# Half-array attention matmuls and seven 256-token Strassen blocks in a fused attention and FFN kernel

## The chip, the cores and the metric

The kernel runs on one core of one Trainium2 chip, as one program in one launch. The metric is the device time of that program in microseconds. A core has TensorE (PE in the profile; its weight loads are listed apart as PEld), VectorE (DVE), ScalarE (ACT), GpSimd (POOL) and SyncE (SP, which issues the DMAs here). PE writes its results to PSUM, eight banks of 128 partitions by 512 float32 numbers.

## The reference, cut to what matters

```python
# q, k, v: (8 batches, 8 heads, 576 positions, 64) float32; omega: (128, 64)
def phi(x):                                   # random features
    proj = np.einsum('bhsd,md->bhsm', x, omega)
    sq = np.sum(x * x, axis=-1, keepdims=True) / 2.0
    h = proj - sq
    h = h - np.max(h, axis=-1, keepdims=True)
    return np.exp(h) / np.sqrt(m)
q_p, k_p = phi(q * scale), phi(k * scale)
kv  = np.einsum('bhsm,bhsd->bhmd', k_p, v)
z   = np.sum(k_p, axis=2)
num = np.einsum('bhsm,bhmd->bhsd', q_p, kv)
den = np.einsum('bhsm,bhm->bhs', q_p, z)[..., None] + 1e-06
x = (num / den)                               # -> 4608 tokens of 8*64 = 512
h = x @ w_in                                  # 512 -> 2048
g = 0.5 * h * (1.0 + erf(h / sqrt(2)))
out = g @ w_out                               # 2048 -> 512
```

All inputs and the output are float32. The term `sq` is the same for all features of a position, so it falls out when the maximum is taken off.

## The kernel before

**Attention units.** The 64 pairs of batch and head are worked off as 32 units of two heads (`units`, four per batch). Units 0 to 7 are plain: their matmuls take float32 operands (`pair`, `shared`, `kv`, `q_trans`, `num_plain`; L566, L573, L598, L636, L646). The other 24 units are split: an operand is kept as a high part and the rest, and products of parts are added. For a split unit, `load_dup` brings k and q in twice, so that one copy of a head's 64 dimensions lies in partitions 0 to 63 and one in 64 to 127, both heads side by side. `x_high` (L776, ACT) rounds all 128 partitions to float32r, and `x_low` (L785, POOL) replaces the lower 64 partitions by the rest. So one matmul over 128 rows adds high and low part. `proj` (L793) makes the features of k, nine matmuls of 256 columns (128 for each part of omega), which `proj_lo` (L797, ACT) and `proj_add` (L803, DVE) add up. `proj_q` (L815) makes those of q, eight matmuls of 288 columns. `q_blocks` (L818, L820), `exps` (L591), `q_back` (L851), `q_high` (L854) and `q_low` (L857) follow. `kv_split` (L897) makes kv and z in float16 parts. `num` (L655) makes numerator and denominator, twelve float32r matmuls of 288 columns per unit; one head's denominators come out above its numerators and the other's below, so `den` (L666, ACT) and `div` (L704, DVE) work on 64 partitions at a time, twice.

**FFN blocks.** The 4608 tokens go through the FFN in 13 blocks, `TBS` (L28): two of 256, ten of 384, one of 256. Block 0 takes float32 operands (L1076, L1102). In the others each product is three float16 matmuls (high by high, high by low, low by high). In a plain block, `mm1` (L1081) makes the hidden layer, 16 chunks of 12 matmuls with the block's tokens as columns, `gelu`, `g_high` (L1089, L1093, ACT) and `g_low` (L1097, DVE) make the parts of the result, and `mm2` (L1105 to L1107) multiplies by w_out, 48 matmuls of 512 columns for each 128 tokens. From block 9 on (`n0=9`: three of 384 tokens, one of 256), the first product is Strassen's in Winograd's form: seven products instead of eight of half the tokens by half the weights (`WHICH`, `w_prod`, L1294), with sums in PSUM (`c_sum`, L1307) and `w_mm2` (L1392 to L1394) for the second product. `w_prod` has half a block's tokens as columns, so 192 or 128.

**Order.** All operations are put into a `Planner`, which runs a list schedule with costs in microseconds, due times and tables of offsets (`STARTS`, `UDUE`, `OFF`), and emits one fixed order for each engine; an engine takes its instructions in that order. Attention units are fed in among the FFN blocks that come before the block that needs them. PSUM's eight banks are three rings: `acc` (three, second product), `h` (two, first product) and `at` (three, attention; in the Strassen blocks also their sums, `wr`).

Of the kernel before, what the change touches and what calls it, by code (L numbers as in the profile page):

```python
# [19 lines left out]
P = 128  # L20
T = 384
KSC = 2.0 ** 15
TINY = 1e-30
LAG = 2
TOP = 12
TBS = (256, 256) + (384,) * 10 + (256,)

X = dict(fb=1875.39, fbp=-594.94, fb0=-100.43, fbb=-85.01, fbw=8.75, pm=0.081, tsw=1.28, wmaxp=0, plain=8, kvp=8, eb0=8,  # L28
         ttr=1, pair=0, amax=63, qm=1, xm=0, km=0, prelu=0, n0=9, h=2, at=3, vs=5, wr=('h', 'at'), tx=4, ss=4, xh=8, gh=3,
         xp=0, qs=0)  # L30
# [3 lines left out]
STARTS = (-608.76, -310.19, 1013.97, 411.45, 613.3, 691.46, 1509.94, 850.35, 1239.92, 423.8, 1230.35, 1650.1, 1806.11,  # L34
          2438.49)
UDUE = (-1835.47, 171.94, -234.99, -505.01, 748.03, 1179.69, 3047.74, -146.1, -767.14, 900.21, 68.96, 2288.49, -294.59,
# [4 lines left out]
OFF = dict(b_high=-72.2, b_low=149.89, b_sum=1036.96, block_be=-107.12, block_high=221.4, block_low=-34.61,  # L41
           block_out=133.15, block_scales=552.27, block_spread=241.34, bound_a=61.51, bound_b=190.66, bound_c=-206.74,
           c_gelu=585.14, c_high=449.81, c_low=-623.5, c_low22=-1100.56, c_sum=205.13, chain_a=-306.63, chain_b=-159.63,
           chain_c=-20.0, chain_d=-212.25, den=17.46, div=-80.04, exp_tiles=752.95, exps=-624.6, g_high=-17.63,
           g_low=681.68, gelu=134.14, identity=-186.13, k_high=160.56, k_low=-326.52, k_shift=158.24, kv=-341.75,
           kv_a=-532.4, kv_b=-581.5, kv_b2=112.12, kv_c=86.33, kv_d=-195.75, kv_split=0.29, kvz_plain=362.33,
           load_dup=24.33, load_om=-374.68, load_two=-636.72, load_v=79.48, load_vst=733.3, mm1=151.18, mm2=960.95,
           nothing=772.2, num=-1.25, num_plain=152.14, p2=44.04, pair=30.95, proj=-73.32, proj_add=-20.84, proj_lo=-1064.92,
           proj_q=-79.55, q_back=299.04, q_blocks=91.52, q_copy=-909.26, q_high=70.66, q_low=-32.77, q_max=104.46,
           q_max2=-71.57, q_max3=-83.93, q_max4=-451.32, q_max5=-143.98, q_max6=390.66, q_shift=14.7, q_trans=-186.45,  # L50
           rcp=-223.48, s_high=197.71, s_low=-146.15, s_sum=214.23, s_sum2=35.14, scale_om=55.95, shared=-372.74,
           shift_tiles=-70.18, split_om=993.71, store=-152.29, store_dma=923.2, top=-95.1, v_a=100.77, v_b=111.57,
           v_max=90.81, v_scales=239.24, v_spread=-1125.26, w_abs=757.07, w_hi=-597.71, w_high=301.17, w_lo=320.3,
           w_load=239.07, w_low=35.09, w_max=36.92, w_mm2=-5.42, w_prod=11.49, w_round=138.68, w_seed=390.89,
           w_shift=-223.02, w_sign=-65.79, w_snap=253.45, warm=-115.6, wchain_a=0.47, wchain_b=-558.98, wchain_c=89.3,
           wchain_d=945.01, wchain_e=-544.08, wchain_f=348.34, x_high=-9.09, x_low=138.92, zeros=126.31)
# [7 lines left out]
class Planner:  # L64
# [45 lines left out]
    def run(self, lat, hop, alloc, put):  # L110
# [117 lines left out]
def favor_attention_ffn(ctx: ExitStack, tc: tile.TileContext, qT, kT, v, omT, w_in, w_out, out):  # L228
# [7 lines left out]
    TB = TBS  # L236
# [30 lines left out]
    ones = cp.tile([1, P], F32, name="ones")  # L267
    vta = cp.tile([P, 2, NV, D + 1], F32, name="vt")
# [8 lines left out]
    xf = xt.rearrange("p a h s -> p (a h s)")  # L277
# [10 lines left out]
    pair_at = [xsb[:, 0:2 * T], xsb[:, 2 * T:4 * T], flat0[:, VO:VO + 2 * T], flat0[:, VO + 2 * T:VO + 4 * T], xaf[:, 0:2 * T], xaf[:, 2 * T:4 * T]]  # L288
    pair_at += [w32f[:, 1, c:c + 2].rearrange("p c w -> p (c w)")[:, 0:2 * T] for c in (0, NF // 2)]
    pair_at = [t.rearrange("p (j t) -> p j t", j=2) for t in pair_at]  # L290
    tx_at = [flat0[:, VO + (4 + i) * T:VO + (5 + i) * T] for i in range(3)] + [xaf[:, 4 * T:5 * T]]
# [10 lines left out]
                vsc=2, bs=4, be=2, tx=X['tx'], ss=X['ss'], raw=2, r=2 if X['xm'] else 3, lo=2, qt=2, ql=2 if X['qm'] else 4, kvh=1, kvl=1, xh=X['xh'], xl=X['xh'], gh=X['gh'], gl=X['gh'], o=2)  # L302
    for k, b in bufs.items():
# [103 lines left out]
    def w_lo(pc):  # L407
        nc.scalar.activation(pc.l or raw(pc)[1], raw(pc)[1].bitcast(U32), AF.Copy, scale=2.0 ** -29)
# [78 lines left out]
    def weights_in(win, i):  # L487
# [4 lines left out]
        op('ACT', 1.08, w_lo, pc, r=[rk], w=pc.lk if pc.l is not None else [rk + ('lo',)])  # L492
# [13 lines left out]
    def weights_scale(win):  # L506
# [33 lines left out]
    def ek(u, t):  # L540
# [3 lines left out]
        return [('eq', u.eb, g) for g in range(a // HS, b // HS + 1)]  # L544
# [64 lines left out]
    def sums(u):  # L609
# [3 lines left out]
        if u.kp:  # L613
            pv = kv_out(u)
            return pv[:, :, 0:D], pv[:, :, D:D + 1]
        kz = G['kvz', u].rearrange("p a (b d) -> p (a b) d", d=D)
        return kz[:, 0:4:3], kz[:, 1:3, 0:1]

    def bound_a(u):
        nc.scalar.activation(G['zr', u], sums(u)[1], AF.Copy, bias=TINY)  # L620
# [909 lines left out]
```

## Time and profile before

| What | us |
|---|---|
| median of three runs | 984.22 (981.91 to 984.6) |
| profiled execution, its own time | 984.64 |
| its span, first to last instruction | 982.9 |
| TensorE busy in the span | 951.7 |
| VectorE busy | 768.7 |
| ScalarE busy | 764.7 |
| GpSimd busy | 419.5 |

The profiled execution's own time is 1.7 us above its span. Matmuls are pipelined: a row's duration runs from its start to its modelled end, and overlaps that of the next. What one matmul costs the engine is the distance from its start to the next one's start, read in the timeline. Each row of the timeline has its start, its length, engine, line and operation, what it writes and reads, then rows by columns of the array that are active, then partitions by columns and type. A float32 matmul of the program appears as two records, a float32r or float16 one as one.

### The profile page before, as it was taken

The numbers are of one execution on the slowest core, as the hardware profiler recorded it, in microseconds if no ns is written. First come the engines' busy times: TensorE is split into PE (matmuls) and PEld (weight loads), VectorE is DVE, ScalarE is ACT, GpSimd is POOL, SyncE is SP. The second block draws the span as 40 slices with busy tenths as digits, with TensorE's granted clock in tenths as the row PEclk, the third lists the DMA queues.
The fourth block names the chain that finished last, engine by engine and source line by source line (L and its number), as shares of the span: only waits on it lengthen the run. The fifth ranks groups of instructions, "written<-read, shape, count | busy, mean of one in ns | idle before, by whom it ended". The sixth has DMA issues, their size and how long they took to land.

```text
span 982.9 us, 18957 instructions
## 1 busy us (share of the span) xinstructions
PE 951.7 (97%) x6572; PEld 625.3 (64%) x6572; DVE 768.7 (78%) x2023; ACT 764.7 (78%) x1591; POOL 419.5 (43%) x612
## 2 busy tenths in 40 slices
PE   7988999899999999999999999999999999999998
PEld 5765666656655555565656665665666777767776
DVE  4898998999989997898889986996989575642322
ACT  6998768799899879979799987787779675654453
POOL 2235345666647674752564533552565011220000
PEclk7999999999999999999999999999999999999999
DMA  9774324222213221322213222231111000000000
GB/s 270 219 230 143 131 57 128 63 83 63 63 55 89 76 62 58 82 67 83 62 38 102 66 52 70 62 90 43 50 49 49 10 2 33 2 22 12 1 34 22
DMA packets 46287, 71.01 MB, mean 72 GB/s; under 512 B 13680, under 2 KB 22256, under 8 KB 46192
## 3 DMA queue, kind: packets, MB, share of 16 engines
q1 hardware_dynamic: 46192, 69.81, 24.1%
q8 instruction: 52, 0.85, 0.4%
q14 instruction: 43, 0.35, 0.1%
HBM read 60.36 MB, written 9.44 MB: 71 GB/s over the span
## 4 chain that ended last, share of the span: by engine, by line
PE 68%; DVE 18%; ACT 5%; POOL 3%; issue 2%; DMA 1%; SPq 1%; ACTq 0%; POOLq 0%
PE h L1081 16%; PE h L1294 5%; PE acc L1105 5%; PE acc L1107 5%; PE acc L1106 5%; PE at L1294 5%; PE acc L1393 4%; PE acc L1394 4%; PE acc L1392 4%; PE acc L1102 3%; PE at L655 3%; PE h L1076 2%; DVE gl L1097 2%; PE at L793 2%; PE at L897 2%
## 5 line engine op out<-in xcount | busy, mean ns | idle before, releaser
L785 POOL TENSOR_TENSOR r<-xt,r 64x288 fp32r<-64x288 f32 (+2 forms) x216 | 178.2, 843 | 147.0 <-ACT r L776 107.1
L1081 PE MATMUL h<-xh,wih 128*128 128x384 f16 (+1 forms) x512 | 163.7, 320 | 8.3 <-DVE gl L1097 7.6
L1081 PE MATMUL h<-xl,wih 128*128 128x384 f16 (+1 forms) x512 | 163.7, 320 | 0.0
L1081 PE MATMUL h<-xh,wil 128*128 128x384 f16 (+1 forms) x512 | 163.7, 320 | 0.0
L1105 PE MATMUL acc<-woh,gh 128*128 128x512 f16 x368 | 140.2, 381 | 0.0
L1107 PE MATMUL acc<-wol,gh 128*128 128x512 f16 x368 | 139.5, 379 | 0.0
L1106 PE MATMUL acc<-woh,gl 128*128 128x512 f16 x368 | 139.5, 379 | 0.0
L1081 PEld LDWEIGHTS <-wih 128*128 128x128 f16 x1024 | 97.6, 98 | 55.2 <-issue 0.2
L1097 DVE SCALAR_TENSOR_TENSOR gl<-h,bs,gh 128x384 f16<-128x384 f32 (+1 forms) x128 | 75.6, 590 | 24.9 <-ACT gh L1093 23.5
L776 ACT CAST r<-xt 128x256 fp32r<-128x256 f32 (+2 forms) x216 | 82.2, 407 | 15.6 <-PE at L815 6.8
L1089 ACT ACTIVATE h<-h,bs 128x384 f32<-128x384 f32 (+1 forms) x128 | 69.0, 540 | 25.3 <-PE h L1081 23.9
L1093 ACT ACTIVATE gh<-h,bs 128x384 f16<-128x384 f32 (+1 forms) x128 | 72.3, 566 | 13.1 <-PE acc L1107 9.8
L1081 PEld LDWEIGHTS <-wil 128*128 128x128 f16 x512 | 50.0, 98 | 39.2 <-issue 11.8
L1393 PE MATMUL acc<-woh,gl 128*128 128x512 f16 (+1 forms) x192 | 69.4, 361 | 0.1
L1392 PE MATMUL acc<-woh,gh 128*128 128x512 f16 (+1 forms) x192 | 69.4, 362 | 0.0
L1394 PE MATMUL acc<-wol,gh 128*128 128x512 f16 (+1 forms) x192 | 69.4, 361 | 0.0
L1294 PEld LDWEIGHTS <-w 128*128 128x128 f16 x768 | 60.3, 98 | 11.1 <-issue 0.9
L1107 PEld LDWEIGHTS <-gh 128*128 128x128 f16 x368 | 36.0, 98 | 43.4
L793 PE MATMUL at<-om,r 128*128 128x256 f32 x216 | 53.6, 337 | 2.6 <-POOL r L785 2.0
L1105 PEld LDWEIGHTS <-gh 128*128 128x128 f16 x368 | 35.8, 97 | 31.6 <-issue 0.2
L417 POOL TENSOR_TENSOR w<-w 128x1024 int32<-128x1024 int32 x12 | 28.5, 2375 | 61.9 <-DVE w L414 35.3
L1106 PEld LDWEIGHTS <-gl 128*128 128x128 f16 x368 | 36.1, 98 | 27.2 <-issue 0.3
(285 smaller groups left out, 2549.8 us busy)
## 6 DMA issues: line engine op xcount, KB each, us to landing
xt<-in_kT SPq DMA_DIRECT2D x56, 288.0 KB, 3.9
xt<-in_qT SPq DMA_DIRECT2D x56, 288.0 KB, 3.8
out_x<-o SPq DMA_DIRECT2D x35, 256.0 KB, 2.1
raw<-in_w_in SPq DMA_DIRECT2D x16, 512.0 KB, 5.5
raw<-in_w_out SPq DMA_DIRECT2D x16, 512.0 KB, 4.4
w<-in_v SPq DMA_DIRECT2D x24, 320.0 KB, 3.0
vt<-in_v SPq DMA_DIRECT2D x8, 320.0 KB, 4.7
out_x<-o SPq DMA_DIRECT2D x2, 128.0 KB, 1.7
```

Source lines behind the costliest of these rows:

```text
L776: nc.scalar.copy(G['r', u, x][:, 0:b - a], xf[:, a:b])
L785: nc.gpsimd.tensor_tensor(r, xf[D:, a:b], r, op=ALU.subtract)
L793: nc.tensor.matmul(o[:, t], r[:, t * P:(t + 1) * P], om, start=True, stop=True)
L1081: nc.tensor.matmul(h[:, 0:t], w, (G['xh', n, j], G['xh', n, j], G['xl', n, j])[k][:, 0:t], start=(i == 0), stop=(i == 3 * NJ - 1))
L1097: nc.vector.scalar_tensor_tensor(G['gl', n, c][:, 0:t], G['h', n, c][:, 0:t], G['bs', n][:, 3:4], G['gh', n, c][:, 0:t], op0=ALU.mult, op1 ...
L1105: nc.tensor.matmul(acc, gh[:, s], woh[:, c, c0:c1], start=(c == 0), stop=False)
L1106: nc.tensor.matmul(acc, gl[:, s], woh[:, c, c0:c1], start=False, stop=False)
L1107: nc.tensor.matmul(acc, gh[:, s], wol[:, c, c0:c1], start=False, stop=(c == NF - 1))
L1294: nc.tensor.matmul(b[:, g * h:(g + 1) * h], w, x[:, kt], start=first and k == 0, stop=last and k == 6 * GP - 1, skip_group_check=True)
L1392: nc.tensor.matmul(acc, gh, woh[:, c, c0:c1], start=begin, stop=False)
L1393: nc.tensor.matmul(acc, gl, woh[:, c, c0:c1], start=False, stop=False)
L1394: nc.tensor.matmul(acc, gh, wol[:, c, c0:c1], start=False, stop=end)
```

## The change

A split unit's two heads now lie on the two halves of the partitions, as they come from memory (`load_two` instead of `load_dup`), and the high and the low part in two tiles (`rh`, `rl`) of all 128 partitions. A projection's operands have 64 rows, so it takes one half of TensorE's rows, and the matmuls of the two heads are issued in turn, each head to a PSUM bank of its own. For k there are, per head, four matmuls of 256 columns (the high part by both parts of omega) and four of 128 (the low part by the high part of omega); the 64 positions per head that are left over are made in float32, in a quarter of the array (`proj_mid`). For q there are six of 288 columns per head. The numerators and denominators are made from float16 parts: each matmul has 64 weight columns, takes one half of the array's columns, and the heads are issued in turn; there are 24 of 288 columns per unit instead of 12. Numerators of both heads now fill one bank and denominators another, so `den` and `div` work on 128 partitions, once.

The FFN has blocks of 256, 256, six of 384 and seven of 256 tokens; the last seven are Strassen's, 1792 tokens where it was 1408. Their `w_prod` matmuls have 128 columns, and an operation on the sums takes four chunks (`GP = 4`) and 512 columns at a time. The parts of x have a buffer of their own (`xx`). The planner has new costs, offsets and a table `MOVES` of offsets for single operations, all of which set the order.

The diff, cut to its core (the tables, of which a program makes the order, are shown by their rows below):

```diff
-TBS = (256, 256) + (384,) * 10 + (256,)
+    KP = X['k']
+    N0 = 2 + KP
+    TB = (256, 256) + (384,) * KP + (256,) * ((NTOK - 512 - 384 * KP) // 256)
...
     def num(u, half):
-        for hh in range(2):
-            ps = G['pn', u, half, hh]
+        def one(hh, a):
+            o, w = G['pn', u, half, a][hh * D:(hh + 1) * D, 0:HS], slice(a * D, (a + 1) * D)
+            h, l = (G[z, u][:, hh, w] for z in ('kvh', 'kvl'))
             qh = G['qh', u][:, hh * S + half * HS:hh * S + (half + 1) * HS]
-            ops = [(G['kvh', u], qh), (G['kvl', u], qh), (G['kvh', u], G['ql', u, half][:, hh] if X['qm'] else G['ql', u, 2 * hh + half][:, 0])]
-            for i, (a, c) in enumerate(ops):
-                nc.tensor.matmul(ps[:, 0:HS], a[:, hh], c, start=(i == 0), stop=(i == len(ops) - 1))
+            ql = G['ql', u, half][:, hh] if X['qm'] else G['ql', u, 2 * hh + half][:, 0]
+            return (h, qh, o, True, False), (l, qh, o, False, False), (h, ql, o, False, True)
+
+        for a in (1, 0):
+            matmuls(one(0, a), one(1, a))
...
-        r = G['r', u, x][D:, 0:b - a]
-        nc.gpsimd.tensor_tensor(r, xf[D:, a:b], r, op=ALU.subtract)
+        nc.gpsimd.tensor_tensor(G['rl', u, x][:, 0:b - a], u.x2[:, x // 2, a:b], G['rh', u, x][:, 0:b - a], op=ALU.subtract)
...
+    def part_k(u, hh, x0, w, o):
+        x = int(x0 + w > XR[0][1])
+        r, x0 = slice(hh * D, (hh + 1) * D), x0 - XR[x][0]
+        h, l = (G[z, u, x][r, x0:x0 + w] for z in ('rh', 'rl'))
+        return (h, om[r], o, True, False), (l, om[r, 0], o[:, 0], False, True)
+
+    def matmuls(*rows):
+        for row in zip(*rows):
+            for a, b, o, first, last in row:
+                nc.tensor.matmul(o, a, b, start=first, stop=last, skip_group_check=True)
+
+    def proj(u, x):
+        for y in range(2):
+            c = 2 * x + y
+            matmuls(*[part_k(u, hh, hh * (S % P) + c * P, P, halves(G['pp', u, x, hh])[:, y]) for hh in range(2)])
+
+    def proj_mid(u):
+        w = S % P
+        for hh, x0 in ((0, MID * P), (1, 0)):
+            r = slice(hh * D, (hh + 1) * D)
+            nc.tensor.matmul(G['ps', u][r, 0:P], u.x2[r, 0, x0:x0 + w], om32[r], start=True, stop=True)
...
-    def proj_q(u, g):
-        for i in range(2):
-            nc.tensor.matmul(G['pp', u, NK + g][:, 0:HS], om[:, i], xr_part(u, NK + g), start=(i == 0), stop=(i == 1))
+    def proj_q(u, x):
+        def one(hh):
+            r, o = slice(hh * D, (hh + 1) * D), G['pq', u, x, hh][:, 0:HS]
+            h, l = (G[z, u, 2 + x][r, 0:HS] for z in ('rh', 'rl'))
+            return (om[r, 0], l, o, True, False), (om[r, 1], h, o, False, False), (om[r, 0], h, o, False, True)
+
+        matmuls(one(0), one(1))
...
-    GP = 2
+    GP = 4
...
+    def prime(i):
+        nc.tensor.matmul(G['prime', i], wih[:, 0, 0:P], woh[:, 0], start=True, stop=True)
```

What the order looks like now is shown at three places, all on TensorE, with the lines of each kernel (`proj` was L793 and `proj_q` L815; now both, and `num`, are issued by `matmuls`, L1134; `mm1` was L1081 and is L1423; `mm2` was L1105 to L1107 and is L1447 to L1449). A row with x2 stands for two equal instructions in a row.

The first place is a piece of q's projection among the FFN's matmuls, in a unit in the middle of the attention. Before, it stands so:

```order
L1081 LDWEIGHTS wil
L1081 MATMUL h<-xh,wil 128x384
L815 MATMUL at<-r,om 128x288 x2
L1081 LDWEIGHTS wih
L1081 MATMUL h<-xl,wih 128x384
```

And in the changed kernel so:

```order
L1449 LDWEIGHTS gh
L1449 MATMUL acc<-wol,gh 128x512
L1134 MATMUL at<-rl,om 128x288 x2
L1134 MATMUL at<-rh,om 128x288 x4
L1423 LDWEIGHTS wih
L1423 MATMUL h<-xx,wih 128x384
```

Two matmuls over the whole array have become six over half of its rows, one piece of q being half of both heads where it was half of one; matmuls over the whole array stand before and after them in both.

The second place is a piece of k's projection. Before:

```order
L1081 LDWEIGHTS wil
L1081 MATMUL h<-xh,wil 128x384
L793 MATMUL at<-om,r 128x256 x2
L897 LDWEIGHTS vt
L897 MATMUL at<-vb,vt 128x129
```

In the changed kernel:

```order
L1449 LDWEIGHTS gh
L1449 MATMUL acc<-wol,gh 128x512
L1134 MATMUL at<-om,rh 128x256 x2
L1134 MATMUL at<-om,rl 128x128 x2
L1134 MATMUL at<-om,rh 128x256 x2
L1134 MATMUL at<-om,rl 128x128 x2
L1447 LDWEIGHTS gh
L1447 MATMUL acc<-woh,gh 128x512
```

Here two matmuls for two tiles of one head have become eight for two tiles of both heads, again with the whole array's matmuls on both sides.

The third place is the numerators' end in one half of a unit. Before, all of the half stands in six rows, of which the last four are:

```order
L655 MATMUL at<-ql,kvh 128x288
L655 MATMUL at<-qh,kvh 128x288
L655 MATMUL at<-qh,kvl 128x288
L655 MATMUL at<-ql,kvh 128x288
L1081 LDWEIGHTS wih
L1081 MATMUL h<-xl,wih 128x384
```

In the changed kernel it is twelve matmuls of 64 result partitions, each with a weight load of its own, the two heads in turn; the rows, with the buffers' numbers, end so:

```order
L1134 LDWEIGHTS kvl_3168
L1134 MATMUL at_3340<-qh_3159,kvl_3168 64x288
L1134 LDWEIGHTS kvh_3151
L1134 MATMUL at_3340<-ql_3231,kvh_3151 64x288
L1134 LDWEIGHTS kvh_3151
L1134 MATMUL at_3340<-ql_3231,kvh_3151 64x288
L1423 LDWEIGHTS wih_67
L1423 MATMUL h_3326<-xx_85,wih_67 128x384
```

Over the whole order, TensorE goes from the whole array to a part of it, back, or from one part to another, 60 times before and 383 times now; a stretch on parts of the array, between matmuls on all of it, comes 24 times before, all in plain units, and 180 times now, 156 of them in split units, where 168 (seven for each of 24 units) would be the most. The last attention matmul stood before after 600 of the 1344 matmuls of `w_prod`, and stands now after 1344 of 2352.

More of the change, by code (lines that the diff above doesn't have):

```diff
@@ L41 @@
[L41 to L56, printed above, removed]
@@ L629, in bound @@
     def bound(u, key):
-        op('ACT', 0.12, bound_a, u, r=[key], new=[('zr', ('zr', u))])
+        op('ACT', 0.12, bound_a, u, r=[key] + [('vsc', u.b)] * u.split, new=[('zr', ('zr', u))])
         op('DVE', 0.3, bound_b, u, r=[key], w=[('zr', u)], new=[('km', ('km', u))])
-        op('POOL', 0.2, bound_c, u, r=[('km', u), ('zr', u)], w=[('xm', u.b)])
+        op('POOL', 0.33, bound_c, u, r=[('km', u), ('zr', u)], w=[('xm', u.b)])
     def q_trans(u, g):
@@ L715, in out_ops @@
         ring = ANY if u.mode == 0 else 'at'
-        op('PE', 1.0 if not u.split else 0.8, num if u.split else num_plain, u, half, r=r + rr, w=keys,
+        op('PE', 1.2 if not u.split else 0.8, num if u.split else num_plain, u, half, r=r + rr, w=keys,
            new=[(ring, k) for k in pn])
-        n = 0.5 if not u.split else 0.92
-        op('ACT', n, den, u, half, r=pn + ([('vsc', u.b)] if not u.kp else []), new=[('dt', ('dt', u, half))])
-        op('DVE', 0.92, rcp, u, half, r=[('dt', u, half)], new=[('rt', ('rt', u, half)), ('rc', ('rc', u, half))])
-        c = sum(0.15 + (c1 - c0) / 960 for _, c0, c1, _ in ps) * (2 if u.split else 1)
+        op('ACT', 0.5, den, u, half, r=pn + ([('vsc', u.b)] if not u.kp else []), new=[('dt', ('dt', u, half))])
+        op('DVE', 1.155, rcp, u, half, r=[('dt', u, half)], new=[('rt', ('rt', u, half)), ('rc', ('rc', u, half))])
+        c = sum(0.17 + (c1 - c0) / 900 for _, c0, c1, _ in ps)
         op('DVE', c, div, u, half, due=(2, 2 * u.k + half, 0.0, 0.0), r=pn + [('rt', u, half)], w=keys)
@@ L809, in k_shift, with proj_lo, add, proj_add @@
+    def proj_lo(u, x, hh):
+        nc.scalar.copy(lo_at(u, hh), halves(G['pp', u, x, hh])[:, :, 1])
+    def add(u, t, hi, lo):
+        nc.vector.tensor_tensor_reduce(u.et[:, t], hi, lo, 1.0, -3e38, ALU.add, ALU.max, G['nm', u][:, t:t + 1])
+    def proj_add(u, x, hh):
+        for y in range(2):
+            add(u, hh * (MID + 1) + 2 * x + y, halves(G['pp', u, x, hh])[:, y, 0], lo_at(u, hh)[:, y])
+    def mid_add(u):
+        add(u, MID, G['ps', u][:, 0:P], nil.broadcast_to([P, M]))
     def k_shift(u):
@@ L960, in batch_v @@
             op('SP', 0, load_vst, u, w=[u.vk], size=327e3)
-            op('DVE', 0.8, v_max, u, r=[u.vk], w=[('vm', b)])
+            op('DVE', 0.73, v_max, u, r=[u.vk], w=[('vm', b)])
         chain(b, 0)
-        op('POOL', 0.8, v_scales, b, r=[('exp', b, 0)], new=[('vsc', ('vsc', b))])
-        op('ACT', 0.3, v_spread, b, w=[('vsc', b)])
+        op('POOL', 1.05, v_scales, b, r=[('exp', b, 0)], new=[('vsc', ('vsc', b))])
+        op('ACT', 0.44, v_spread, b, w=[('vsc', b)])
     def split_pre(u):
@@ L995, in split_pre @@
+        op('POOL', 2.14, k_shift, u, r=[nm] + [nm + z for z in ((0, 0), (0, 1), (1, 0), (1, 1), (2,))], w=[('et', u.eb, t) for t in range(NT)])
         mx, mc, nq = ('mx', u), ('mc', u), ('nq', u)
-        qe = [('eq', u.eb, g) for g in range(4)]
-        op('ACT', 0.24, q_max, u, r=[mx] + [('mxg', u, g) for g in range(4)], new=[('mc', mc)])
-        op('DVE', 0.22, q_max2, u, r=[mc], w=[mx])
+        qe = [('eq', u.eb, g) for g in range(QG)]
+        op('ACT', 0.24, q_max, u, r=[mx] + [('mxg', u, g) for g in range(QG)], new=[('mc', mc)])
@@ new lines, in split_post @@
+        op('ACT', 0.74, v_a, u, r=[u.vk, ('vsc', u.b), 'p2'], w=['vb'])
+        op('DVE', 0.85, v_b, u, r=[u.vk, ('vsc', u.b)], w=['vb'])
+        for g in range(len(KG)):
+            es = [('et', u.eb, t) for t in KG[g]]
+            n = len(KG[g])
+            op('POOL', 0.1 + 0.15 * n, k_high, u, g, r=es + ['kk'], w=[('kk', g)])
+            op('DVE', 0.07 + 0.135 * n, k_low, u, g, r=es, w=[('kk', g)])
+        for g in range(len(KG)):
+            op('PE', 0.088 * len(KG[g]), kv_split, u, g, r=['vb', ('kk', g)], w=[] if g == 0 else [pk],
+               new=[('at', pk), ('kvs', ('kvs', u)), ('kvz', ('kvz', u))] if g == 0 else [])
@@ L1035, in split_post @@
+        op('ACT', 0.2, kv_a, u, r=[pk], w=[('kvs', u)])
+        op('DVE', 0.2, kv_b, u, r=[pk, ('kvs', u)], w=[('kvz', u)])
+        op('ACT', 0.39, kv_b2, u, r=[pk], w=[('kvz', u)])
+        op('ACT', 0.31, kv_c, u, r=[('kvz', u)], new=[('kvh', ('kvh', u))])
+        op('DVE', 0.34, kv_d, u, r=[('kvz', u), ('kvh', u)], new=[('kvl', ('kvl', u))])
+        bound(u, ('kvz', u))
         for x, g in enumerate((0, 1) if X['qm'] else (0, 2, 1, 3)):
             c = 0.3 * X['qm']
-            op('DVE', 0.42 + c, q_back, u, g, r=[('eq', u.eb, y) for y in ((g, g + 2) if X['qm'] else (g,))], new=[('qt', ('qt', u, g))])
+            op('DVE', 0.42 + c, q_back, u, g, r=[('eq', u.eb, y) for y in range(QG)], new=[('qt', ('qt', u, g))])
@@ L1321, in c_in @@
     def c_in(n, q, part):
[L1322 removed]
+        return c_src(n, q, part)
     def c_high(n, q, part):
@@ L1418, in block @@
         if is_w(n):
-            for q in range(NF // 2 // GP + 1):
-                if q < NF // 2 // GP:
+            for q in range(NQ + 1):
+                if q < NQ:
                     wino_first(n, q)
```

424 lines of the change are left out of this document (205 added, 219 removed), and 326 rows, old and new, of tables (MOVES, UDUE).

## The prediction

> **What bounds the kernel now.** I read the page first, then busy time by stage, then TensorE's waits, then its timeline matmul by matmul.
>
> ```profile
> span 982.9 us, 18957 instructions
> PE 951.7 (97%) x6572; PEld 625.3 (64%) x6572; DVE 768.7 (78%) x2023; ACT 764.7 (78%) x1591; POOL 419.5 (43%) x612
> ```
>
> TensorE is busy for 97% of the span; the next engine has 78%. A busy TensorE can hide waits, since rows overlap, so the stages come next: the columns are the stretch, its length, then PE, PEld, DVE, ACT and POOL with busy time, the clock, the share of the DMA engines and GB/s. Stage one holds the weights and the plain units, stage two the split units, stage three the FFN alone.
>
> ```profile
> 0.00:98.30 98.30, 83.61 (x615) 60.65 (x616) 78.19 (x175) 82.64 (x176) 34.62 (x32) 0.93 0.71 215
> 98.30:787.00 688.70, 675.60 (x4246) 423.41 (x4245) 604.62 (x1657) 575.25 (x1201) 364.53 (x543) 1.00 0.24 68
> 787.00:982.80 195.80, 192.50 (x1715) 141.28 (x1713) 85.90 (x193) 106.84 (x215) 20.37 (x37) 1.00 0.04 16
> ```
>
> In stage two (clock 1.00), where all that is edited in the attention lies, TensorE idles for 688.7 - 675.6 = 13.1 us. Its waits there, as total, times and longest:
>
> ```profile
> PE h L1081 <- DVE gl L1097: 7.6, 10, 1.7
> PE at L793 <- POOL r L785: 2.0, 2, 1.8
> PE h L1294 <- DVE at L1307: 0.7, 1, 0.7
> ```
>
> So from 98 us on the order of TensorE's work is the time, and no other engine's relief can bring more than about 13 us. Everything turns on what the edits do to TensorE's own work.
>
> **Part 1: Strassen blocks.** Rows of the timeline give start, length, then the matmul; cost is start to start.
>
> ```profile
> 900.42 0.33 PE L1294 MATMUL at<-xh,w 128*128 128x192 f16 x2
> ...
> 901.41 0.38 PE L1392 MATMUL acc<-woh,gh 128*128 128x512 f16 x1
> 901.62 0.38 PE L1393 MATMUL acc<-woh,gl 128*128 128x512 f16 x1
> ...
> 953.49 0.22 PE L1294 MATMUL h<-xh,wih 128*128 128x128 f16 x1
> ...
> 954.16 0.38 PE L1392 MATMUL acc<-woh,gh 128*128 128x512 f16 x1
> ```
>
> Twelve products (one chunk and one of the seven) lie between the first and the second of these rows: 0.99 / 12 = 0.0825 us for 192 columns. Twelve lie between the last two: 0.67 / 12 = 0.056 for 128. One of 512 columns takes 0.21 to 0.22 (0.215 below). A plain matmul of 384 columns takes 0.16:
>
> ```profile
> 222.05 0.33 PE L1081 MATMUL h<-xh,wil 128*128 128x384 f16 x1
> 222.21 0.33 PE L1081 MATMUL h<-xl,wih 128*128 128x384 f16 x1
> 222.37 0.33 PE L1081 MATMUL h<-xh,wih 128*128 128x384 f16 x1
> 222.40 0.53 PE L793 MATMUL at<-om,r 128*128 128x256 f32 x2
> 222.77 0.34 PE L1081 MATMUL h<-xh,wil 128*128 128x384 f16 x1
> ```
>
> Gone: one plain block of 384 (192 x 0.16 + 144 x 0.215 = 61.7) and three Strassen blocks of 384 (336 x 0.0825 + 144 x 0.215 = 58.7 each), 237.8 us. Added: six Strassen blocks of 256 (336 x 0.056 + 96 x 0.215 = 39.45), 236.7. **-1.1 us**: smaller blocks give back, matmul by matmul, nearly all of what the additional 384 tokens save. The two `prime` matmuls add 0.4.
>
> The Trainium skill's page "TensorE: Matmul & The Clock Gate", section "Back-to-back issue gap", states about 81 ns per matmul of 128 columns for sustained pairs of weight load and matmul. The row says 56 ns, with such a load before each; by the page's figure the 2016 additional matmuls of 128 columns (2352 now, 336 before) would make this part an estimated +50 us instead of -1.1.
>
> **Part 2: the split units' matmuls on the whole array, which go.** Between 222.37 and 222.77 lie one of 384 columns and two of L793: (0.40 - 0.16) / 2 = 0.12 us each.
>
> ```profile
> 264.24 0.38 PE L1107 MATMUL acc<-wol,gh 128*128 128x512 f16 x1
> 264.26 0.48 PE L655 MATMUL at<-qh,kvh 128*128 128x288 f32 x1
> ...
> 265.24 0.43 PE L815 MATMUL at<-r,om 128*128 128x288 f32 x2
> 265.51 0.39 PE L1105 MATMUL acc<-woh,gh 128*128 128x512 f16 x1
> ```
>
> Here eight of 288 columns (six of L655, two of L815) take 265.51 - 264.24 - 0.215 = 1.055, 0.132 each. A unit has 9 x 0.12 + 20 x 0.132 = 3.72 us, 24 units 89.3. The first of a group starts 0.02 to 0.03 after the matmul ahead of it: entering and leaving such a group costs nothing extra.
>
> **Part 3: the same on halves of the array.** The trace before has halves only in plain units: column halves in L646, row halves in L566, all float32.
>
> ```profile
> 156.97 0.27 PE L1081 MATMUL h<-xl,wih 128*128 128x256 f16 x1
> 157.18 1.19 PE L646 MATMUL at<-qh,kvz 128*64 128x288 f32 x8
> 158.30 1.12 PE L1102 MATMUL acc<-w,gh 128*128 128x512 f32 x2
> 159.26 0.38 PE L1105 MATMUL acc<-woh,gh 128*128 128x512 f16 x1
> ...
> 88.07 1.16 PE L566 MATMUL at<-om,xt 64*128 64x128 f32 x16
> 89.17 0.70 PE L1076 MATMUL h<-xa,w 128*128 128x256 f32 x2
> ```
>
> A column streams in 0.16 / 384 = 0.00042 us, and a float32 record streams its columns twice (two records of 512 take 0.96 from 158.30: four times 0.215, and 0.1 for a load). Eight records of 288 would need 8 x 0.242 = 1.94 one after the other; they take 1.12. Sixteen of 128 would need 1.72; they take 1.10. So the two halves do run side by side: 4 x 0.242 = 0.97 and 8 x 0.1075 = 0.86. But 0.15 and 0.24 us are left over, and the entry is late as well: the last matmul ahead streams until 156.97 + 0.11 = 157.08, and the half's first starts at 157.18, 0.10 later. The weight loads show why:
>
> ```profile
> 157.17 0.68 PEld L646 LDWEIGHTS at<-qh,kvz 128*64 128x64 f32 x8 [0.21 <-issue]
> 158.29 0.30 PEld L1102 LDWEIGHTS acc<-w,gh 128*128 128x128 f32 x2 [0.44 <-issue]
> ```
>
> Between whole array and halves, no load starts while the other still streams. **A stretch on halves therefore costs a fixed 0.25 us (columns) or 0.34 us (rows) over its streams.** The page "TensorEngine Tiling (Array Packing)" of the Trainium skill, section "Key Properties", names it: "Changing tiling mode (not just tile) drains the TensorE". It gives no price and excepts no type, so by it the new float16 and float32r groups pay as these do.
>
> A new unit, by stretch: `proj` streams 256, 128, 256, 128 columns, both heads at once. For the first 128 I take 0.108, the step of L566, which loads as many float32 weight columns; with nothing but its stream it would be 0.054. So about 0.39, plus 0.34, twice. `proj_q` 3 x 0.121, and up to 0.132 as before: 0.38 + 0.34, twice. `num` 6 x 0.122 = 0.74 + 0.25, twice. `proj_mid` 0.22 + 0.25. Sum: 1.46 + 1.44 + 1.98 + 0.47 = 5.35 us, of which 2.1 are entries and exits; 24 units 128.4. The order merges 12 of 168 stretches, which I put at 2 us. 126.4 - 89.3 = **+37 us**.
>
> **Part 4: the other engines.**
>
> ```profile
> L785 POOL TENSOR_TENSOR r<-xt,r 64x288 fp32r<-64x288 f32 (+2 forms) x216 | 178.2, 843 | 147.0 <-ACT r L776 107.1
> L776 ACT CAST r<-xt 128x256 fp32r<-128x256 f32 (+2 forms) x216 | 82.2, 407 | 15.6 <-PE at L815 6.8
> L666 ACT ACTIVATE dt<-at,vsc 64x288 f32<-64x288 f32 x96 | 47.6, 496 | 5.6 <-PE at L655 3.2
> L704 DVE TENSOR_TENSOR xa<-at,rt 64x160 f32<-64x160 f32 (+1 forms) x48 | 17.0, 354 | 0.8
> ```
>
> `x_low` and `x_high` fall from 216 to 96 each (some 95 us on POOL, 40 on ACT), `den` from 96 to 48 (24 on ACT), `div` to half, and the doubled loads of k and q go, from DMA engines 24% busy. All of it lies beside a TensorE that is busy 98% of stage two, so it earns nothing itself; were that cover gone, DVE at 604.6 of 688.7 us would be next. What it can earn is in the waits: of the 13.1 us I let 8 go, as DVE has less to do per us of TensorE. Added is one kind of wait: `proj` and `num` need two of the ring `at`'s three banks at once, also beside Strassen blocks (about 29% of the attention's matmuls now), whose sums hold one. Behind a waiting `proj` on TensorE stand the FFN's matmuls, and behind those ACT's gelu. The bound from above is 49 stretches of 0.7 (the one such wait seen, L1294 on L1307), 34 us; from below nothing. I take 2, since that row shows one in all. Stage one and the last store (3.3 us idle in stage three) stay.
>
> **Sum.** -1.1 + 0.4 + 37 - 8 + 2 = +30.3 on the profiled execution's 984.64 us (0.4 above the median shown): **1015 us**.
>
> **Rivals.**
> *Free switches, faster.* The left-over 0.25 to 0.34 us belong to float32, and a float16 or float32r load for a half starts under the stream ahead, as in part 2. For it: no half in the trace is of these types, and L793 enters after 0.03. Against it: at 157.18 float16 goes over to halves and waits all the same. Price: streams alone are 2 x (0.39 + 0.38 + 0.74) + 0.22 = 3.24 us a unit, -11.5 in all; with -0.7 and the waits' -6, 966 us. It decides where a stretch costs under 18.2 / 156 = 0.117 us instead of 0.25 to 0.34.
> *No halves side by side.* The new types run one after the other, so the change doesn't do what it says: streams of `proj`, `proj_q` and `num` double, 24 x 3 = +72, 1087 us. Only the types speak for it; both rows of part 3 show overlap.
> *Loads that bind.* In the last block 128 columns are paired with loads for one block; over seven blocks, beside attention, the loads could fail to hide.
>
> ```profile
> L1294 PEld LDWEIGHTS <-w 128*128 128x128 f16 x768 | 60.3, 98 | 11.1 <-issue 0.9
> ```
>
> A load takes 0.098 us; shown in full it makes 0.098 of each 0.056, 2016 x 0.042 = +85, 1100 us. The row at 953.49 speaks against it: there it is hidden, twelve times in a row. The skill page's figure of part 1 lies between the two.
>
> **How the numbers follow.** Forecast 0.82, free switches 0.11, a stretch near 0.117 and so no change 0.02, no overlap 0.03, loads that bind 0.02. The forecast's own range: all waits of stage two gone and none added (-7), 128 columns at 0.054 (-3), loads of 64 float16 columns shorter (-3) give 1002; no wait saved (+8) and bank waits of 10 give 1031. It holds nine tenths of its 0.82; to reach 0.8 it is stretched to 988 (a switch cheaper by a half or so) and 1038. Slower 0.87, within 0.3% (about what a measurement of this kernel can tell from no change) 0.02, faster 0.11.
>
> **What would show it.** Right: TensorE's share stays at 97% or more and the time grows anyway; in the timeline a group of L1134 starts 0.1 us after the stream ahead ends, and the next whole-array matmul 0.1 after it; two heads start within 0.01 us; 0.056 per `w_prod`; the wait on `gl` under 4 us. Wrong: groups of L1134 that start 0.03 us after the matmul ahead (free switches); pairs 0.1 apart (no overlap); new PE waits on `at` of over 10 us.

## The result, and the profile after

| | before | after |
|---|---|---|
| time, us (median) | 984.41 (981.91 to 986.45) | 1019.7 (1018.41 to 1019.9) |
| span of the profiled execution, us | 982.9 | 1016.5 |

The change makes the kernel slower: ratio 1.0353, 95% interval 1.033 to 1.0377. Each experiment below was measured in a set with runs of the kernel before (medians 984.8 to 985.0 us), and its ratio is to those. The profile's page of the kernel after begins with the span and the busy time of each engine:

```profile
span 1016.5 us, 21076 instructions
PE 983.6 (97%) x8038; PEld 615.3 (61%) x8038; DVE 741.1 (73%) x1937; ACT 693.3 (68%) x1362; POOL 329.2 (32%) x524
```

Every engine except TensorE does less than before (VectorE 741 against 769 us, ScalarE 693 against 765, GpSimd 329 against 420), and the kernel takes 35 us more (33.6 by the spans). TensorE is still busy for 97%, now with 8038 matmuls instead of 6572. Busy time by stage, columns as in the prediction (length, PE, PEld, DVE, ACT, POOL, clock, DMA). The split units end at some 892 us now, so the cuts differ from those of before; the second row is a stretch that needs a look of its own:

```profile
98.30:760.00 661.70, 658.26 (x4871) 382.96 (x4869) 525.09 (x1429) 471.39 (x928) 234.84 (x379) 1.00 0.15 47
760.00:820.00 60.00, 50.70 (x480) 33.21 (x480) 51.05 (x154) 44.09 (x95) 36.33 (x61) 0.89 0.09 30
820.00:1016.50 196.50, 192.04 (x2127) 138.22 (x2124) 91.11 (x200) 100.21 (x177) 24.75 (x52) 1.00 0.04 15
```

Up to 760 us TensorE idles for 661.70 - 658.26 = 3.4 us, where stage two before had 13.1 in all. Then 60 us hold 9.3 us of idleness, at a clock of 0.89. So the time went to two places: into TensorE's own work, spread over the split units, and into one hole.

**The spread part.** The timeline of TensorE shows a `proj` group and, further on, a `num` group (start, length, matmul; "x2" puts two matmuls into one row; in the rows of L1134 they are the two heads, which start 0.003 to 0.004 us apart):

```profile
302.40 0.33 PE L1423 MATMUL h<-xx,wih 128*128 128x384 f16 x1
302.65 0.38 PE L1134 MATMUL at<-om,rh 64*128 64x256 f32 x2
302.88 0.22 PE L1134 MATMUL at<-om,rl 64*128 64x128 f32 x2
302.93 0.33 PE L1134 MATMUL at<-om,rh 64*128 64x256 f32 x2
303.10 0.22 PE L1134 MATMUL at<-om,rl 64*128 64x128 f32 x2
303.26 0.34 PE L1423 MATMUL h<-xx,wih 128*128 128x384 f16 x1
...
337.22 0.49 PE L1423 MATMUL h<-xx,wih 128*128 128x384 f16 x2
337.64 0.31 PE L1134 MATMUL at<-qh,kvh 128*64 128x288 f16 x2
...
338.27 0.29 PE L1134 MATMUL at<-ql,kvh 128*64 128x288 f16 x2
338.50 0.34 PE L1423 MATMUL h<-xx,wil 128*128 128x384 f16 x1
```

The matmul of 384 columns at 302.40 streams until 302.56. The group starts at 302.65, 0.09 later; its last pair streams 0.054 from 303.10, and the next whole-array matmul starts 0.11 after that. The group costs 303.26 - 302.56 = 0.70 us. For `num` the two matmuls that begin at 337.22 end at 337.54, and the group costs 338.50 - 337.54 = 0.96, with 0.10 to 0.11 of nothing on either side. Its six rows step by 0.12 us, the stream of one matmul of 288 columns, so the two heads of a row do run side by side. Over 45 `proj` groups and 43 `num` groups the medians are 0.70 and 0.95 us.

Two other groups, `proj_q` and `proj_mid`, stand further on:

```profile
772.36 0.38 PE L1727 MATMUL acc<-wol,gh 128*128 128x512 f16 x1
772.67 0.40 PE L1134 MATMUL at<-rl,om 64*128 64x288 f32 x2
772.91 0.43 PE L1134 MATMUL at<-rh,om 64*128 64x288 f32 x4
773.27 0.39 PE L1725 MATMUL acc<-woh,gh 128*128 128x512 f16 x1
...
774.36 0.38 PE L1727 MATMUL acc<-wol,gh 128*128 128x512 f16 x1
774.66 0.44 PE L1145 MATMUL at<-om,xt 64*64 64x128 f32 x4
775.03 0.39 PE L1725 MATMUL acc<-woh,gh 128*128 128x512 f16 x1
```

In the same way `proj_q` costs 773.27 - 772.36 - 0.215 = 0.69 us and `proj_mid` 775.03 - 774.36 - 0.215 = 0.46.

**The hole.** Of TensorE's waits after 98 us, these are the largest (total, times, longest):

```profile
PE h L1423 <- DVE gl L1439: 2.3, 3, 0.9
PE at L1134 <- ACT dt L1003: 1.4, 1, 1.4
PE h L1637 <- ACT xx L1603: 1.2, 1, 1.2
PE at L1134 <- DVE nm L1154: 1.1, 1, 1.1
PE acc L1726 <- DVE gl L1669: 1.1, 1, 1.1
PE h L1637 <- DVE at L1650: 1.1, 1, 1.1
```

The first is the wait of 7.6 us of before. The other five are single events between 779 and 807 us. The timeline there shows the last product of one Strassen block, attention groups far apart, and the first product of the next block (the brackets give the idle time ahead and what ended it):

```profile
775.47 0.38 PE L1727 MATMUL acc<-wol,gh 128*128 128x512 f16 x1
...
779.40 0.78 PE L1134 MATMUL at<-om,rh 64*128 64x256 f32 x2 [1.13 <-DVE nm L1154]
...
781.54 0.45 PE L1134 MATMUL at<-qh,kvl 128*64 128x288 f16 x2 [0.53 <-DVE kvl L1262]
...
785.61 0.60 PE L1134 MATMUL at<-rl,om 64*128 64x288 f32 x1 [1.38 <-ACT dt L1003]
...
787.50 0.45 PE L1134 MATMUL at<-qh,kvh 128*64 128x288 f16 x2 [0.82 <-DVE xa L1050]
...
790.37 0.26 PE L1637 MATMUL h<-xx,wih 128*128 128x128 f16 x1 [1.21 <-ACT xx L1603]
```

From 775.7 to 790.4 us TensorE has no FFN matmul at all. The next block's tokens come from a batch whose last units are still in the attention. Three of the groups wait for a bank of `at` that `proj_add`, `den` or `div` still reads (779.40, 785.61, 787.50: 3.3 us together); others wait for operands, as at 781.54 for `kvl`, and the next block waits for its tokens. The chain of work that ended last has no piece of TensorE from 770.06 to 791.28: of these 21 us VectorE has 13.5, ScalarE 4.7, GpSimd 1.4. Two of its longest pieces are an exponential on ScalarE and transposes of q on VectorE:

```profile
781.69 2.03 ACT w L931
783.75 1.44 DVE qt L1210 x2
```

So in the hole TensorE is held by the other engines' work on the last units, partly through the banks. I had looked for bank waits spread thinly beside Strassen blocks; those that there are sit in this one place.

### The profile page after: what moved, and what is told of

Same layout as the page of the kernel before. It is cut to its first block, busy times and chain, and to the rows that moved or that the text cites. A ratio compares the mean times of both kernels' runs of the same rounds, so it can differ in the third digit from the quotient of the medians.

```text
span 1016.5 us, 21076 instructions
## 1 busy us (share of the span) xinstructions
PE 983.6 (97%) x8038; PEld 615.3 (61%) x8038; DVE 741.1 (73%) x1937; ACT 693.3 (68%) x1362; POOL 329.2 (32%) x524
## 4 chain that ended last, share of the span: by engine, by line
PE 76%; DVE 11%; ACT 9%; issue 2%; POOL 1%; DMA 1%; SPq 0%; ACTq 0%; POOLq 0%; DVEq 0%
PE h L1423 18%; PE at L1134 8%; PE h L1637 6%; PE acc L1447 6%; PE acc L1448 6%; PE acc L1449 6%; PE at L1637 5%; PE acc L1725 5%; PE acc L1726 5%; PE acc L1727 5%; PE at L1241 2%; DVE xx L1606 1%; PE acc L1444 1%; PE h L1418 1%; ACT raw L741 1%
## 5 line engine op out<-in xcount | busy, mean ns | idle before, releaser
L1423 PE MATMUL h<-xx,wih 128*128 128x384 f16 (+1 forms) x896 | 221.8, 319 | 2.4 <-DVE gl L1439 2.3
L1423 PE MATMUL h<-xx,wil 128*128 128x384 f16 (+1 forms) x448 | 142.8, 319 | 0.0
L1120 POOL TENSOR_TENSOR rl<-xt,rh 128x320 fp32r<-128x320 f32 (+1 forms) x96 | 86.8, 912 | 149.3 <-ACT rh L1112 148.3
L1447 PE MATMUL acc<-woh,gh 128*128 128x512 f16 x320 | 121.7, 380 | 0.0
L1449 PE MATMUL acc<-wol,gh 128*128 128x512 f16 x320 | 121.3, 379 | 0.0
L1423 PEld LDWEIGHTS <-wih 128*128 128x128 f16 x896 | 85.6, 98 | 52.8 <-issue 6.0
L1725 PE MATMUL acc<-woh,gh 128*128 128x512 f16 (+1 forms) x240 | 87.7, 365 | 0.3 <-ACT gh L1666 0.3
L1112 ACT CAST rh<-xt 128x320 fp32r<-128x320 f32 (+1 forms) x96 | 42.6, 445 | 37.5 <-PE at L1134 28.3
L1423 PEld LDWEIGHTS <-wil 128*128 128x128 f16 x448 | 43.8, 98 | 29.5 <-issue 5.2
L1637 PEld LDWEIGHTS <-wih 128*128 128x128 f16 x672 | 53.8, 99 | 3.5 <-issue 2.2
L1637 PE MATMUL h<-xx,wih 128*128 128x128 f16 x544 | 52.4, 222 | 2.2 <-ACT xx L1603 1.2
L1449 PEld LDWEIGHTS <-gh 128*128 128x128 f16 x320 | 31.3, 98 | 37.8
L1637 PE MATMUL at<-xx,w 128*128 128x128 f16 x864 | 53.6, 219 | 0.0
L1447 PEld LDWEIGHTS <-gh 128*128 128x128 f16 x320 | 31.1, 97 | 32.4 <-issue 5.9
```

Of the source, the lines that this page charges most:

```text
L1120: nc.gpsimd.tensor_tensor(G['rl', u, x][:, 0:b - a], u.x2[:, x // 2, a:b], G['rh', u, x][:, 0:b - a], op=ALU.subtract)
L1423: nc.tensor.matmul(h[:, 0:t], w, (G['xh', n, j], G['xh', n, j], G['xl', n, j])[k][:, 0:t], start=(i == 0), stop=(i == 3 * NJ - 1))
L1447: nc.tensor.matmul(acc, gh[:, s], woh[:, c, c0:c1], start=(c == 0), stop=False)
L1449: nc.tensor.matmul(acc, gh[:, s], wol[:, c, c0:c1], start=False, stop=(c == NF - 1))
L1637: nc.tensor.matmul(b[:, g * h:(g + 1) * h], w, x[:, kt], start=first and k == 0, stop=last and k == 6 * GP - 1, skip_group_check=True)
L1725: nc.tensor.matmul(acc, gh, woh[:, c, c0:c1], start=begin, stop=False)
```

## Experiments

### Numerators back on the whole array

```
-            o, w = G['pn', u, half, a][hh * D:(hh + 1) * D, 0:HS], slice(a * D, (a + 1) * D)
-            h, l = (G[z, u][:, hh, w] for z in ('kvh', 'kvl'))
+            o = G['pn', u, half, a][:, 0:HS]
+            h, l = (G[z, u][:, a] for z in ('kvh', 'kvl'))
...
         for a in (1, 0):
-            matmuls(one(0, a), one(1, a))
+            matmuls(one(1 - a, a))
...
```

A group is 6 matmuls on 128x128 instead of 12 on halves. Further lines give kv and z the layout in memory that this needs.

> The changed kernel, in which `num` alone goes back to the whole array: 6 float16 products of 288 columns on 128x128 instead of 6 pairs on column halves, in the same places of the same order (heads get each other's numerators, so this shows time, not values). Streams stay at 6 x 0.122 us. Switch theory (a stretch on column halves costs about 0.21 us beyond its streams, the trace of the changed kernel has 0.95 us for such a group): 48 x 0.18 to 0.22, 9 to 10.5 us less, 1009 to 1011 us. Rival (half-array groups cost no more than their streams; the loss comes from waits): within 0.3% of 1019.7, 1017 to 1023 us.

Measured: 1011.73 us (1008.9 to 1012.53), ratio to before 1.0263 (1.0245 to 1.0281): 8.0 us less than the kernel after, and 0.7 above the forecast interval. The timeline of this run, at the group that stood at 337.64:

```profile
337.82 0.49 PE L1423 MATMUL h<-xx,wih 128*128 128x384 f16 x2
338.15 0.29 PE L1134 MATMUL at<-qh,kvh 128*128 128x288 f16 x1
...
338.76 0.29 PE L1134 MATMUL at<-ql,kvh 128*128 128x288 f16 x1
338.88 0.33 PE L1423 MATMUL h<-xx,wil 128*128 128x384 f16 x1
```

The two matmuls ahead end at 338.14, the group starts at 338.15, and the next starts 0.12 after its last: 0.74 us for the same streams that cost 0.96 on halves. Over 48 groups that is 10.6 us; 8 arrived, and where the rest went was not followed. The rival, that halves cost only their streams, is out.

### All three groups on the whole array

```
...
-        return (h, om[r], o, True, False), (l, om[r, 0], o[:, 0], False, True)
+        return G['rl' if hh else 'rh', u, x][:, x0:x0 + w], om, o, True, True
...
-        matmuls(one(0), one(1))
+        o = [G['pq', u, x, hh][:, 0:HS] for hh in range(2)]
+        h, l = (G[z, u, 2 + x][:, 0:HS] for z in ('rh', 'rl'))
+        matmuls(((om[:, 0], l, o[0], True, True), (om[:, 1], h, o[1], True, False), (om[:, 0], h, o[1], False, True)))
```

The first pair is in `part_k` of `proj`, the rest in `proj_q`; `num` is as above, and `proj` issues its two matmuls per tile as one row.

> As the run with `num` on the whole array, and `proj` and `proj_q` too: 4 float32r products of 256 columns and 3 of 288 on 128x128 in the same places (heads are mixed, so this shows time, not values; `proj` streams 0.11 us more than its halves do). Only `proj_mid` and the plain units stay on halves. Switch theory: `proj` 0.70 to 0.48, `proj_q` 0.69 to 0.40, `num` 0.95 to 0.73 us, 48 x 0.73 = 35 us less, 985 us; up to 10 us of it may turn into waits on VectorE, which a faster TensorE meets earlier, so 983 to 997 us. Rival (waits are the cause): 1017 to 1030 us.

Measured: 991.79 us (991.05 to 993.82), ratio to before 1.0072 (1.0055 to 1.0089): 27.9 us less than after. That is 79% of the loss, by the shape of the matmuls: the groups stand in the same places and write the same banks. TensorE idles more than it did, 7.6 us from 98.3 to 745 us against 3.4 in the kernel after, which takes part of the forecast 35 back; the largest wait of this run between 98 and 745 us:

```profile
PE h L1419 <- DVE gl L1435: 4.3, 5, 1.7
```

### Heads one after the other

```
-        for row in zip(*rows):
+        for row in rows:
             for a, b, o, first, last in row:
```

> The changed kernel with the two heads' matmuls one head after the other inside each group, instead of in turn; nothing else differs. If matmuls start in program order and only neighbours on different halves overlap: `num` has 9 instead of 6 steps of 0.121, `proj_q` 5 instead of 3, `proj` some 0.2 us more: about 0.8 us a pair of stretches, twice a unit, 24 units, +38 us, 1058 us (1045 to 1070). If the halves run by themselves whatever the order: 1018 to 1025 us. If nothing overlaps in this order: +72, 1092 us.

Measured: 1021.13 us (1019.61 to 1022.22), ratio 1.0362 (1.0347 to 1.0378), against 1.0353 for the kernel after: no difference. The theory that I gave first (matmuls start in program order) misses by 37 us, the second holds. In this run's timeline the heads overlap in pairs all the same:

```profile
303.66 0.40 PE L1134 MATMUL at<-om,rh 64*128 64x256 f32 x2
303.89 0.24 PE L1134 MATMUL at<-om,rl 64*128 64x128 f32 x2
303.95 0.34 PE L1134 MATMUL at<-om,rh 64*128 64x256 f32 x2
304.12 0.23 PE L1134 MATMUL at<-om,rl 64*128 64x128 f32 x2
304.28 0.34 PE L1423 MATMUL h<-xx,wih 128*128 128x384 f16 x1
```

In the program the rows read 256, 128 for one head, then 256, 128 for the other; on the chip they run as 256 and 256, 128 and 128, at most 0.02 us apart. Each half takes its own matmuls without waiting for the other's place in the program, so the one fixed order of an engine holds for TensorE's matmuls within a half, not between the two. The Trainium skill's page "TensorEngine Tiling (Array Packing)", section "Key Properties", says that tiles operate independently and can load and multiply in parallel; this run agrees, and adds that the order between halves inside a group is free.

### Halves where nothing else is touched

```
         nc.tensor.matmul(acc, gh, woh[:, c, c0:c1], start=begin, stop=False)
-        nc.tensor.matmul(acc, gl, woh[:, c, c0:c1], start=False, stop=False)
-        nc.tensor.matmul(acc, gh, wol[:, c, c0:c1], start=False, stop=end)
+        for s in (slice(0, D), slice(D, P)):
+            nc.tensor.matmul(acc[s], gh[:, s], wol[:, c, c0:c1], start=False, stop=False, skip_group_check=True)
+        nc.tensor.matmul(acc, gl, woh[:, c, c0:c1], start=False, stop=end)
```

> The kernel before, in whose Strassen blocks each accumulation of the second layer has its product gh x wol as two column halves side by side (512 columns each, 64 rows of the result each) between two whole-array products: the same streams, 192 more stretches on halves, in blocks where TensorE waits for nearly nothing; no attention is edited. Switch theory: 0.21 to 0.25 us each, 40 to 48 us more, 1024 to 1033 us. Rival (float16 halves enter and leave for free): 982 to 988 us.

Measured: 1027.51 us (1026.87 to 1027.88) against 985.04 for the kernel before in the same set, ratio 1.0428 (1.0412 to 1.0443). That is 42.5 us for 192 stretches, **0.221 us each**. The timeline gives the same for one:

```profile
959.77 0.38 PE L1392 MATMUL acc<-woh,gh 128*128 128x512 f16 x1
960.08 0.41 PE L1394 MATMUL acc<-wol,gh 128*64 128x512 f16 x2
960.42 0.39 PE L1395 MATMUL acc<-woh,gl 128*128 128x512 f16 x1
```

From the end of the first stream (959.77 + 0.215 = 959.985) to 960.42 there are 0.435 us, of which 0.215 are streams. So the price belongs to the halves, for float16 too, and to no part of the attention.

### Float16 numerators alone, in two forms

Both are the kernel before with `ql`, `kvh`, `kvl` and `qh` in float16 on the whole array; they differ in where the batch's scale is applied. The lines below show that place alone; with the scale in `den`, `bound_a` takes a scale from a tile too and `kv_b2` takes none.

```
-    kinds = dict(raw=I32, r=F32R, ql=F32R, kvh=F32R, kvl=F32R, ...)
+    kinds = dict(raw=I32, r=F32R, ql=F16, kvh=F16, kvl=F16, ...)
     # first form, in den:
+    nc.scalar.activation(dt[r], ps, AF.Identity, bias=G['vsc', u.b][r, 1:2], scale=G['vsc', u.b][r, 2:3])
     # second form, in den, as before:
     nc.scalar.activation(dt[r], ps, AF.Identity, bias=G['vsc', u.b][r, 1:2])
```

> The kernel before with one part of the change alone: numerators in float16 (scales as in the changed kernel), but on the whole array, with heads, projections, blocks and order as before. No stretch on halves is added. Switch theory: twelve products of 288 columns a unit go from 0.132 to about 0.122 us, 24 x 12 x 0.010 = 2.9 us less, 982 us (980 to 984). Rival (the new types themselves cost, by their loads or casts): 985 us or more.

Measured: 989.63 us (988.76 to 990.62), ratio 1.005 (1.0035 to 1.0066): slower, where I had forecast faster. The time is the rival's.

> The kernel before with float16 numerators on the whole array again, but with ScalarE's `den` left as it was (a bias and no scale for each row: the batch's scale goes into the values beforehand, as before). In the run that scaled in `den`, TensorE's numerator groups got 2.6 us shorter as forecast, `den` went from 496 to 587 ns in 96 calls, and the time rose by 5. Theory (the longer `den` holds banks and operands, and TensorE waits for them): without it 981 to 984 us. Rival (something else of float16 delays TensorE, its operands on VectorE or its loads): 988 to 991 us again.

Measured: 983.83 us (983.29 to 985.41), ratio 0.9994 (0.9985 to 1.0003): in the forecast interval, at its upper end, and not to be told from before. The groups of `den` in the two runs, first form and second (count, busy time, mean ns of one):

```profile
L669 ACT ACTIVATE dt<-at,vsc 64x288 f32<-64x288 f32 x96 | 56.4, 587 | 5.3 <-PE at L658 2.8
```

```profile
L669 ACT ACTIVATE dt<-at,vsc 64x288 f32<-64x288 f32 x96 | 47.6, 496 | 5.4 <-PE at L658 2.9
```

A scale taken from a tile makes each call 91 ns longer. That is 8.7 us on an engine that is busy for 78% of the span, and the kernel takes 5.8 us more with it. `bound_a` and `kv_b2` change too, but their sums on ScalarE cancel (2.0 us more and 2.2 less). So float16 itself costs nothing here; by which waits ScalarE's delay reaches TensorE was not followed.

### Another bank for U

```
-    new=[] if b in bank else [(WR[p == 5], b)]
+    new=[] if b in bank else [(('acc' if p == 5 else 'h') if n < NBLK - 1 else WR[p == 5], b)]
```

`UDUE`, `STARTS`, `OFF` and `MOVES` are set anew with it. The order differs everywhere, not at the hole alone.

> The changed kernel with the sums of Strassen products 5 and 3 (the bank U) in the ring `acc`, of whose three banks blocks of 256 tokens use two, instead of in the ring `at`, in all blocks but the last; W stays in `h` there; the tables of due times are set anew for it. Matmuls, groups and stretches are the same in kind and number. The trace of the changed kernel has TensorE idle or waiting some 13 us between 775 and 810 us, before the block whose tokens the attention has not finished. Theory (attention beside Strassen blocks is held up by the banks of `at`, two at once for every group): that stretch goes, 8 to 12 us less, 1008 to 1012 us. Rival (it is VectorE's load and the length of the last unit's chain, whatever the banks): within 0.4% of 1019.7, 1016 to 1024 us. By both, the loss to the switches stays, so it stays slower than before.

Measured: 1009.63 us (1007.37 to 1010.39), ratio 1.0251 (1.0231 to 1.027): 10.1 us less than after. Stretches of 20 us, first of the kernel after, then of this run:

```profile
760.00:780.00 20.00, 18.32 (x123) 9.18 (x123) 15.11 (x55) 11.72 (x26) 9.59 (x13) 1.00 0.17 57
780.00:800.00 20.00, 14.38 (x143) 10.55 (x143) 17.89 (x55) 14.36 (x37) 15.24 (x35) 0.66 0.09 31
```

```profile
760.00:780.00 20.00, 20.00 (x221) 13.49 (x219) 16.33 (x48) 18.25 (x41) 8.85 (x27) 1.00 0.01 2
780.00:800.00 20.00, 19.09 (x203) 12.79 (x202) 17.89 (x48) 10.89 (x26) 9.03 (x10) 1.00 0.18 58
```

The hole is gone, with VectorE as busy as before (17.89 of 20 us in both), so VectorE's load alone was not the cause. The number of stretches on parts of the array is not the cause either: the trace of this run has seven more than that of the kernel after. That it was the bank, and not the new order, is not shown: the run changes both, and the bank waits in the hole of the kernel after come to 3.3 us, not 10. The Trainium skill's page "TensorEngine Tiling (Array Packing)", section "Gotcha 1: PSUM Pressure", warns that row tiling raises the pressure on PSUM, since different row tiles write to different banks; the trace agrees as far as its two bank waits of groups on row halves go, 1.1 and 1.4 us.

### Both causes away

This is the kernel of the last section with the whole-array groups of the second run.

> Both causes taken away at once: the kernel with the bank U in `acc` (1009.6 us), in which `num`, `proj` and `proj_q` run on the whole array as in the run with all three (values mixed between heads, `proj` with 0.11 us more of streams). Theory (switches and the banks beside Strassen blocks are all of the loss): 1009.6 - 28 = 982 us, 978 to 988, no slower than before. Rival (a third cause is left): 990 us or more.

Measured: 980.29 us (979.86 to 982.74), ratio to before 0.9961 (0.9948 to 0.9973). The groups give 29.3 us here (27.9 above), the bank with its order 11.5 (10.1 above). No third cause is needed for the 35 us. Its heads are mixed, so it weighs the causes and is no version to use. No run points to one that beats both kernels: the nearest, float16 numerators with `den` as before, is the same as the kernel before.

## Why the prediction was right, point by point

**The bound.** The order of TensorE's work is the time: right up to 760 us, where the relief of VectorE, ScalarE and GpSimd earned most of what the waits had held (3.4 us idle, of 13.1 in stage two before). In the hole it is wrong: there the other engines' work on the last units is the time.

**Part 1, blocks.** Right in its rows. Beside the attention, 24 products of 128 columns run from the first of these rows to the second, 1.35 / 24 = 0.056 us each:

```profile
830.73 0.23 PE L1637 MATMUL h<-xx,wih 128*128 128x128 f16 x1
...
832.08 0.38 PE L1725 MATMUL acc<-woh,gh 128*128 128x512 f16 x1
```

So "loads that bind" is out, and the -0.7 us for blocks and `prime` stands by these rows; no run measured it by itself.

**Parts 2 and 3, the groups.** Right, a little too dear. Forecast 0.73, 0.72, 0.99 and 0.47 us for `proj`, `proj_q`, `num` and `proj_mid`, found 0.70, 0.69, 0.96 and 0.46. A unit costs 2 x 2.35 + 0.46 = 5.16 instead of 5.35, so the term is 24 x 5.16 - 2 - 89.3 = +33 instead of +37. The runs with whole-array groups gave back 28 to 29. The fixed part, 0.25 for columns, was measured at 0.221; 0.34 for rows comes to 0.31 with the prediction's own streams of 0.39 and 0.38. "Free switches" falls with the runs on the whole array and with the halves in the FFN; "no halves side by side" falls with the six rows of `num`, two heads in each, that step by 0.12 us. The signs that the prediction gave for itself are all there: a share of 97%, 0.09 to 0.11 us on either side of a group, two heads within 0.004 us, the wait on `gl` at 2.3 us. Of the signs of being wrong, the waits on `at` after 98 us stay at 6 us, under the 10 that it named.

**Part 4, the other engines.** The -8 for waits is right outside the hole: 3.4 us of idleness to 760 us against 631.70 - 620.84 = 10.9 before in a like stretch:

```profile
98.30:730.00 631.70, 620.84 (x3806) 384.54 (x3805) 560.74 (x1563) 531.71 (x1122) 341.10 (x514) 1.00 0.25 72
```

The +2 for banks was too small. The run with another bank gained some 10 us, inside the bound of 34 that the prediction kept; as bank waits the trace shows 3.3. The step that failed there is "since that row shows one in all": a single wait in a trace where the last attention matmul stands after 600 matmuls of `w_prod` was taken as the rate for one where it stands after 1344. The cover that it counted on, "All of it lies beside a TensorE that is busy 98% of stage two", is gone in one place: at the boundary of a block whose tokens the attention still owes, the other engines' work is not beside a busy TensorE but ahead of it. How the 10 us divide between the banks, the order and that work stays open. By the parts: -0.7 + 33 - 7.5 + 10 = +35; the spans differ by 33.6. The group term was 4 us too large and the bank term 8 too small. That they cancel in part is luck, and brought 1015 within 5 us of what was measured.

## What to carry to other kernels

Before two half-array matmuls replace whole-array ones, count how often the array changes between whole and halves: here each stretch cost 0.22 to 0.31 us over its streams, and the streams that it saved were worth 0.07 us (11.5 us by the prediction's rows, over 168 stretches), so by these figures halves pay only in long runs or where they save much more; no run here has such a case. Look as well at what the next block needs and how far the work for it has come: here a block waited for the last attention units, and a run with another bank and another order closed that hole. And the relief of engines that are not the bound is worth at most the idle time of the one that is, which a profile gives before anything is built.

## What was not expected of the hardware

- The order between two halves in the program does not matter, inside groups of 6 to 12 matmuls: 1021.1 us with the heads one after the other, 1019.7 in turn.
- In the hole the granted clock falls. It is 0.66 on the mean from 780 to 800 us in the kernel after, and 1.00 in the same stretch of the run with another bank, so part of what the hole costs is paid in matmuls that run at a lower clock. In the timeline a pair of `num` steps on by 0.24 us there (782.21, 782.45), against 0.12 elsewhere:

```profile
782.21 0.45 PE L1134 MATMUL at<-qh,kvh 128*64 128x288 f16 x2
782.45 0.45 PE L1134 MATMUL at<-qh,kvl 128*64 128x288 f16 x2
```

- ScalarE's activation on 64x288 takes 587 ns with a scale from a tile and a bias, 496 with the bias alone. The changed kernel's `den` has such a scale too (585 ns on 128x288, 48 calls), so it saves ScalarE 19.5 us and not the 24 of the prediction.
